# A fixed program order for four engines in the attention phase of an attention and two-MoE kernel

## The chip, the core and the metric

One core of one Trainium2 chip runs the whole kernel. It has a matrix engine (TensorE, "PE" in the rows, with its weight loads as "PEld"), a vector engine (VectorE, "DVE"), a scalar engine (ScalarE, "ACT"), GpSimd ("POOL") and SyncE ("SP", which here only issues DMAs). Each engine works through its own list of instructions in the order in which the built program has them, and waits at an instruction until its inputs and its output buffer are ready. The metric is the device time of one run in microseconds (us), lower is better.

## What is computed

Three blocks follow one another: top-32 attention over 4 batches, 8 heads and 576 positions (head size 64), a dense feed-forward block with a hard gate, and a sparse block of 8 experts with two experts per token. All is fp32.

```python
scores = scale * q @ k.T
kth = np.partition(scores, -32, axis=-1)[..., -32:-31]
attn = softmax(where(scores >= kth, scores, -1e9))
x = (attn @ v), laid out as 2304 tokens x 512
h = x @ w_in                       # 512 -> 2048
x = (h * clip(h + 3, 0, 6) / 6) @ w_out
logits = x @ w_gate + log1p(exp(x @ w_noise)) * noise
out = sum over the two best experts of weight * (relu(x @ w1[e]) @ w2[e])
```

## The kernel before, in words

`phase_a` does the attention and the dense block together, `phase_b` the experts. The 2304 query rows are 18 tiles of 128; a tile and a head make one "slot" of work, 144 in all, and the loop `for st in range(-6, end)` at the end of `phase_a` is a software pipeline over slots. In its step `st` it calls, each for another slot: the key and query transposes and their copies (`k_trans`, `kq_trans`, `k_evac`, `q_evac`) for slot st; the scores on PE and their copy to SBUF on ACT (`scores`, `s_evac`) and seven segment maxima on DVE (`seg`, L313) for slot st-1; the threshold search over the segment maxima (`chain`, L319 to L323), the bias for the exponential on POOL (`nbias`) and the mask (`zmask`, L340) for st-2; the product of mask and scores on POOL (`ysum`, L346) and the exponential on ACT for st-3; the exact 32nd value (`ymax` L352, `select` L356) and the masked sum (`pmask`, L365, `recip`) on DVE for st-4; the transposes of the result on PE (`ptrans`, with `ptevac` on ACT) for st-5; the product with the values (`av`, one call per two heads) for st-6; and the scaling and rounding of the result (`xscale`, `xsplit`) later.

The dense block runs in the same loop as "units": a chunk of 256 tokens and one of 16 blocks of 128 hidden columns. There are 144 units, one per step from step 25 on, so the last 25 run after the attention. A unit is `mm1` (12 matmuls into one PSUM bank, tile `h`), `hrelu` on ACT, `hgate` on DVE (L478), and in the next step `hround` on ACT, `hlow` on POOL (L491) and `mm2` (6 matmuls, tile `xa`). Bank `h` exists once: `mm1` of a unit waits for `hgate` of the unit before. Its weights arrive as 64-bit numbers. In the steps 4 to 19 one block of them per step is converted (`convert`, four DVE instructions, L117 and L118 twice, one on ACT, one on POOL) and split (`split`: PE and ACT); 11 of the 16 blocks are written back and streamed again for every chunk.

The keys of a batch and head are loaded, split and transposed once, shortly before the first slot that needs them (`ksched`): heads in 4 runs of 8 steps. As a batch has 4.5 tiles, 16 slots (tiles 4 and 13) hold rows of two batches and need twice the score matmuls.

When the last units of a chunk are done, the routing for the experts (`make_route`) comes as a list of small closures of which a few are called at the end of each step; `logits` are 4 transposes and `logits2` the small matmuls that follow, one of them per step, four steps a chunk.

What sets the order: the kernel is recorded in the order of the loop, but the tile framework's scheduler then builds each engine's list by its own model of time and by priorities. Two places guide it by hand: `av` raises the priority of its matmuls (`AVP_AHEAD`) and `after` chains a few instructions. Ring sizes are the constants at the top (`KTB` for transposed keys, `VB` for values, `VL` the step at which values are loaded); PSUM is full, each tag once.

Of the kernel before, what the change touches and what calls it, by code (L numbers as in the profile page):

```python
# [30 lines left out]
WD = 2  # L31
WP = 16
LAG = 10
AVP_AHEAD = 150
ZB = 2
OS, OA, OB, OC, OD, OE, OV, OX, OY = 1, 1, 2, 3, 4, 5, 6, 8, 10
VL = 4
SSB = 4

ONV = ''  # L40
# [2 lines left out]
BEGIN = 12  # L43
KRB = 2
LXB = 2
VB = 9
XMB = 2
QRB = 2
GB = 2
KTB = 10  # L50
PHB = 2
SEGB = 3
A8B = 4
# [87 lines left out]


def phase_a(tc, pools, ident, q, k, v, w_in, w_out, X, thrs, wscr, stream, begin, on_chunk=None, slots=NSLOT, pace=None):
    nc = tc.nc
    wp, ap, mp, ps, dr = pools
    TS, TT, STT = nc.vector.tensor_scalar, nc.vector.tensor_tensor, nc.vector.scalar_tensor_tensor

# [48 lines left out]
    KT, V = {}, {}  # L196

    KR, KS = {}, {}

    def k_load(i):  # L200
        dl, b, h = ksched[i]
        KR[i] = kr = ap.tile([128, 5, 64], F32, name=f"kr{i}", tag="kr", bufs=KRB)
        nc.sync.dma_start(kr[:, 0:4, :], k[b, h, 0:512, :].rearrange("(p j) d -> p j d", j=4))
        nc.sync.dma_start(kr[0:64, 4, :], k[b, h, 512:576, :])

    def k_split(i):

        kr = KR.pop(i)
        KS[i] = ks = ksb[i % KSB]
        for sl in ((slice(0, 128), slice(0, 4)), (slice(0, 64), slice(4, 5))):  # L210
            hi, lo = ks[sl[0], sl[1], 0, :], ks[sl[0], sl[1], 1, :]
            copy('k', hi, kr[sl])
            nc.gpsimd.tensor_tensor(lo, kr[sl], ks.bitcast(F32)[sl[0], sl[1], 0, :], op=ALU.subtract)

    def v_load(i):
        dl, b, h = ksched[i]
        vt = ap.tile([128, 5, 64], F32, name=f"v{i}", tag="v", bufs=VB)
        nc.sync.dma_start(vt[:, 0:4, :], v[b, h, 0:512, :].rearrange("(p j) d -> p j d", j=4))
        half = slice(64 * (h % 2), 64 * (h % 2) + 64)
        nc.sync.dma_start(vt[half, 4, :], v[b, h, 512:576, :])  # L220
        other = 64 - 64 * (h % 2)
        nc.gpsimd.memset(vt[other:other + 64, 4, :], 0.0)
        V[b, h] = vt

    KP, QP = {}, {}

    def k_trans(i):
        ks = KS[i].rearrange("p j a d -> p j (a d)")
        pm = ps.tile([128, 512], F32, name=f"kp{i}", tag="pa")
        for j in range(4):  # L230
            flip(nc, pm[:, j * 128:(j + 1) * 128], ks[:, j, :], identr)
        KP[i] = pm

    def kq_trans(i, t):
        pm = ps.tile([128, 512], F32, name=f"qp{i}_{t}", tag="misc")
        if t is not None:
            qs = QS[divmod(t // 4, 2)][:, t % 4].rearrange("p a d -> p (a d)")
            flip(nc, pm[:, 0:128], qs[:, 0:128], identr)
            flip(nc, pm[:, 128:256], qs[:, 128:256], identr)
            QP[t] = pm  # L240
        if i is not None:
            ks = KS.pop(i)[:, 4].rearrange("p a d -> p (a d)")
            flip(nc, pm[:, 256:384], ks, identr)
            KP[i] = (KP[i], pm)

    def k_evac(i):
        dl, b, h = ksched[i]
        KT[b, h] = kt = ap.tile([128, 576], F32R, name=f"kt{i}", tag="kt", bufs=KTB)
        p0, p1 = KP.pop(i)

        m, r = (0, 512) if h % 2 == 0 else (64, 0)
        copy('K', kt[:, m:m + 512], p0)
        copy('K', kt[:, r:r + 64], p1[:, 256:320])
# [138 lines left out]
    def ptevac(i):  # L392
        p = PP.pop(i)
        if i % 2:
            p, half = p
            PH[i // 2] = ap.tile([128, 128], F32, name=f"ph{i}", tag="pth", bufs=PHB)
            first = nc.scalar.copy(PH[i // 2], half)  # L397
        PT[i] = ap.tile([128, 4, 128], F32, name=f"pt{i}", tag="ptt", bufs=PTB)
        last = nc.scalar.copy(PT[i], p.rearrange("p (a n) -> p a n", a=4))
        if i % 2: after(tc, last, first)  # L400

    PH = {}
    AVP, RP, XS, XT = {}, {}, {}, {}
# [1 line left out]
    def av(p):  # L405

        t = p // 4
        AVP[p] = o = ps.tile([128, 512], F32, name=f"av{p}", tag="av")
        prev = None
        with tc.high_priority(AVP_AHEAD):  # L410
            for b, row, n, s0 in pieces(t):
                for j in range(5):
                    for hh in (1, 0):
                        half = slice(64 * hh, 64 * hh + 64)
                        vt, pt = V[b, (2 * p + hh) % 8][:, j, :], PT[2 * p + hh][:, j, :] if j < 4 else PH[p]
                        m = nc.tensor.matmul(o[half, row:row + n], vt, pt[:, row:row + n], start=(j == 0),  # L416
                                             stop=(j == 4), skip_group_check=True)
                        if prev: after(tc, m, prev)
                        prev = m
            m = nc.tensor.transpose(o[:, 128:256], RB.pop(p).rearrange("p a b -> p (a b)"), ident)  # L420
            after(tc, m, prev)
# [110 lines left out]
    wstep = {}  # L532
    for fb in range(NFB):
        wstep.setdefault(W0 + fb * WD // 2, []).append(fb)
    kdl = {dl: i for i, (dl, b, h) in enumerate(ksched)}
    for st in range(-6, end):
        if st == -6: q_load(0, 0)
        if st == BEGIN: begin()
        if st % 4 == 0 and 0 < st // 4 + 1 < slots // 4: q_load(*divmod(st // 4 + 1, 2))
        if st % 4 == 2 and 0 <= st // 4 + 1 < slots // 4: q_split(*divmod(st // 4 + 1, 2))  # L540
        for i, (dl, b, h) in enumerate(ksched):
            if max(dl - 3, min(i, 2) - 6) == st: k_load(i)
            if max(dl - 1, min(i, 2) - 5) == st: k_split(i)
            if dl + VL == st: v_load(i)
        for fb in wstep.get(st + 2, []): wk.load(fb)

        while fetched < len(units) and units[fetched][0] <= st + 3:
            w_fetch(units[fetched][1]); fetched += 1
        u, up = ustep.get(st), ustep.get(st - 1)
        s_, a, b, c, d, e, av_, x1, x2 = (st - x for x in (OS, OA, OB, OC, OD, OE, OV, OX, OY))  # L550
        if ok(x1) and x1 % 2 == 0: xscale(x1 // 2)
        if up:
            hround(up)
            hlow(up)
        if ok(c):
            ysum(c)
            expo(c)
        if u:
            mm1(u)
            hrelu(u)  # L560
        if ok(s_): scores(s_)
        if ok(e): ptrans(e)
        if ok(s_): s_evac(s_)
        if ok(e): ptevac(e)
        ki = kdl.get(st)
        if ki is not None: k_trans(ki)
        if ki is not None or ok(st):
            kq_trans(ki, st if ok(st) else None)
        if ki is not None: k_evac(ki)
        if ok(st): q_evac(st)  # L570

        ch = chain(b) if ok(b) else []
        segs = [(a, j) for j in range(NSEG)] if ok(a) else []
        if ok(d): ymax(d)
        if ch:
            ch.pop(0)()
            nbias(b)
        if ok(d): select(d)
        while ch:
# [681 lines left out]
```

## Time and profile before

| what | us |
|---|---|
| median of three runs (lowest 1414.99, highest 2076.86) | 1418.17 |
| the profiled execution, its own time | 1414.92 |
| its span in the profile | 1413.0 |
| PE busy in the span | 1301.9 |
| VectorE busy in the span | 1000.8 |
| GpSimd busy in the span | 828.6 |
| ScalarE busy in the span | 744.6 |

All times of the trace count from the start of the span; 1.9 us of the execution lie outside it. The attention's last mask ends just before 836 us, the experts follow from about 906 us. A busy share is an average over stages: PE's and VectorE's shares are close to full in the attention, and VectorE's falls behind it.

### The profile page before, as it was taken

The page shows a single profiled execution, that of the slowest core. Times are in us where ns is not written, and L with a number is a line of the kernel's source. Part 1 is how long each engine was busy: PE and PEld are TensorE (multiplying, and loading weights), DVE is VectorE, ACT ScalarE, POOL GpSimd, SP SyncE. Part 2 cuts the span into 40 slices and gives each one's busy share as a digit, 9 for nine tenths or more (in the row PEclk, how much of TensorE's full clock was granted, in tenths as well). Part 3 has the DMA queues.
Part 4 walks back from the last instruction along what each step waited for, and adds up shares of the span by engine and source line. Part 5 has one row for each costly group of instructions (what it writes and reads, how often), then busy time and mean ns, then how long its engine had stood idle before and what let it go on. Part 6 is the DMA issues. An engine that isn't in the chain of part 4 may idle for free.

```text
span 1413.0 us, 26990 instructions
## 1 busy us (share of the span) xinstructions
PE 1301.9 (92%) x9006; PEld 1129.0 (80%) x9006; DVE 1000.8 (71%) x3805; ACT 744.6 (53%) x1565; POOL 828.6 (59%) x1173
## 2 busy tenths in 40 slices
PE   5767899999999979999899999799999999999996
PEld 3545688988888868898688888677989888888985
DVE  7999997899998899986899973345453534444241
ACT  6767766677676756666676654244322322223220
POOL 7665666666666778665577864234414556465461
PEclk8789999999999989999999999999999999999999
DMA  8766645445345614445233547556546556474431
GB/s 244 257 237 226 239 171 193 146 152 172 130 178 191 223 14 156 164 168 200 70 128 137 149 148 256 174 173 224 168 137 195 169 172 192 140 222 163 145 121 38
DMA packets 138100, 239.56 MB, mean 170 GB/s; under 512 B 39779, under 2 KB 93155, under 8 KB 123872
## 3 DMA queue, kind: packets, MB, share of 16 engines
q1 hardware_dynamic: 127600, 210.57, 45.2%
q0 software_dynamic: 10352, 27.18, 5.8%
q8 instruction: 73, 1.20, 0.4%
q14 instruction: 75, 0.61, 0.1%
HBM read 209.08 MB, written 31.64 MB: 170 GB/s over the span
## 4 chain that ended last, share of the span: by engine, by line
PE 56%; DVE 26%; POOL 5%; ACT 4%; DMA 4%; issue 3%; SPq 1%; POOLq 0%; DVEq 0%; ACTq 0%
PE hb L876 15%; PE ac L896 15%; PE h L463 8%; PE xa L503 7%; DVE seg L313 5%; DVE e L365 5%; DVE a L352 4%; DVE z L340 3%; PE s L295 3%; PE av L416 3%; PE pa L384 2%; DVE a L356 2%; DMA kr<-in_k_dram 1%; POOL idw L756 1%; DVE r L478 1%
## 5 line engine op out<-in xcount | busy, mean ns | idle before, releaser
L896 PE MATMUL ac<-w,hh 128*128 128x512 f32 x960 | 247.5, 400 | 4.6 <-ACT hh L881 4.5
L876 PE MATMUL hb<-xe,w 128*128 128x320 f32 (+2 forms) x1536 | 239.4, 310 | 1.1 <-DVE xe L846 0.4
L876 PEld LDWEIGHTS hb<-xe,w 128*128 128x128 f32 x1536 | 231.7, 189 | 9.9 <-issue 3.0
L346 POOL TENSOR_TENSOR y<-z,ss 128x576 f32<-128x576 bf16 x144 | 192.4, 1337 | 57.6 <-DVE z L340 51.3
L896 PEld LDWEIGHTS ac<-w,hh 128*128 128x128 f32 x960 | 173.1, 188 | 43.8 <-ACT hh L881 8.4
L882 DVE SCALAR_TENSOR_TENSOR hh<-hb,hh 128x640 fp32r<-128x640 f32 (+2 forms) x72 | 53.9, 749 | 211.2 <-ACT hh L881 199.7
L881 ACT ACTIVATE hh<-hb 128x640 fp32r<-128x640 f32 (+2 forms) x72 | 46.6, 647 | 293.1 <-PE hb L876 270.2
L313 DVE MAX8 seg<-ss 128x8 f32<-128x82 f32 (+1 forms) x1008 | 166.8, 228 | 21.0 <-ACT ss L304 20.6
L463 PE MATMUL h<-xT,ws 128*128 128x256 f32 x1188 | 164.5, 287 | 7.6 <-DVE r L478 7.4
L503 PE MATMUL xa<-ws,g 128*128 128x512 f32 x594 | 165.8, 403 | 0.0
L463 PEld LDWEIGHTS h<-xT,ws 128*128 128x128 f32 x1188 | 149.6, 190 | 15.1 <-DVE r L478 12.6
L862 POOL TENSOR_TENSOR w<-r,w 128x1024 fp32r<-128x1024 f32 x40 | 98.2, 2462 | 85.1 <-ACT w L860 77.7
L365 DVE SCALAR_TENSOR_TENSOR e<-ss,thrs,e 128x576 f32<-128x576 f32 x144 | 141.7, 984 | 0.5
L335 ACT ACTIVATE e<-ss,a 128x576 f32<-128x576 f32 x144 | 114.0, 792 | 34.4 <-POOL a L328 33.3
L304 ACT COPY ss<-s 128x576 f32<-128x576 f32 x144 | 92.6, 643 | 66.1 <-PE s L389 47.1
L352 DVE MAX8 a<-y 128x8 f32<-128x576 f32 x144 | 108.0, 750 | 25.0 <-POOL y L346 24.8
L491 POOL TENSOR_TENSOR g<-r,g 128x256 fp32r<-128x256 f32 x124 | 96.5, 778 | 36.5 <-ACT g L187 23.2
L340 DVE TENSOR_SCALAR_CACHE_REDUCE z<-ss,a 128x576 bf16<-128x576 f32 x144 | 115.3, 801 | 1.0
L384 PE MATMUL pa<-ident,e 128*128 128x128 f32 x576 | 93.2, 286 | 24.7 <-DVE e L365 21.1
L503 PEld LDWEIGHTS xa<-ws,g 128*128 128x128 f32 x594 | 102.1, 188 | 14.7 <-POOL g L491 0.5
L295 PE MATMUL s<-kt,qt 128*128 128x288 f32 x512 | 102.3, 324 | 8.7 <-ACT ph L397 4.2
L913 POOL DMA_INDIRECT out_dram<-y,id x40 | 42.3, 1058 | 104.1 <-DVE y L912 82.5
(195 smaller groups left out, 2655.3 us busy)
## 6 DMA issues: line engine op xcount, KB each, us to landing
ws<-wscr SPq DMA_DIRECT2D x99, 1024.0 KB
r<-in_moe_w_dram SPq DMA_DIRECT2D x144, 256.0 KB
wscr<-wsp SPq DMA_DIRECT2D x11, 1024.0 KB
wraw<-in_moe_w_in_dram SPq DMA_DIRECT2D x16, 512.0 KB
wraw<-in_moe_w_out_dram SPq DMA_DIRECT2D x16, 512.0 KB
ck<-in_moe_w_in_dram SPq DMA_DIRECT2D x32, 256.0 KB
ck<-in_moe_w_out_dram SPq DMA_DIRECT2D x32, 256.0 KB
out_dram<-zero SPq DMA_DIRECT2D x18, 256.0 KB
```

The costliest lines, as they stand in the source:

```text
L295: nc.tensor.matmul(p[:, half, 0:288], qt[:, j, :], KT[b, h][:, half * 288:(half + 1) * 288], start=(m == 0), stop=(m == n - 1))
L313: nc.vector.max(ST[i][:, j, :], SS[i][:, edge[j]:edge[j + 1]])
L335: nc.scalar.activation(e, SS[i], AF.Exp, bias=A8[i][:, 24:25], scale=0.125)
L340: TS(z, SS[i], A8[i][:, 7:8], None, op0=ALU.is_lt, op1=ALU.add, accum_out=A8[i][:, 26:27])
L346: nc.gpsimd.tensor_tensor(y, Z.pop(i), SS[i], op=ALU.mult)
L352: nc.vector.max(A8[i][:, 8:16], Y.pop(i))
L365: STT(E[i], SS.pop(i), thrs[:, i:i + 1], E[i], op0=ALU.is_ge, op1=ALU.mult, accum_out=SUM[i // 2][:, i % 2:i % 2 + 1])
L384: nc.tensor.transpose(p[:, j * 128:(j + 1) * 128], e[:, j * 128:(j + 1) * 128], ident)
L463: nc.tensor.matmul(p[:, 0:n], w[:, a, d, :], xt[b][:, d, 0:n], start=(m == 0), stop=(m == 11))
L503: nc.tensor.matmul(ACC[t], g[:, a, j * 128:(j + 1) * 128], w[:, b, :], start=(fb == 0 and m == 0), stop=(fb == NFB - 1 and m == 2))
L876: nc.tensor.matmul(p[:, half, 0:hn], w[:, a, d, :], XE[job][:, b, d, half * hn:(half + 1) * hn], start=(m == 0), stop=(m == 11))
L896: o = nc.tensor.matmul(ACC[job, j], h[:, a, j * 128:(j + 1) * 128], w[:, b, :], start=(f == 0 and m == 0), stop=(f == NF2 - 1 and m == 2))
```

## The change

`phase_a` gets its engines from a wrapper, `Lanes`. Each of PE, DVE, ACT and POOL is a `Lane` that adds an ordering edge from every instruction to the one recorded before it on the same engine, so that in `phase_a` (and in the weight conversion that it calls) the scheduler can no longer reorder them. Only SP's DMAs and the closures of `make_route` stay free and are placed between them. The calls in a step are laid out anew: scores first, then the first matmuls of a unit; keys are split two steps ahead, transposed one step ahead (`kdl` has `dl - 1`, `k_trans` after `mm2`) and loaded four ahead; values are loaded one step later; `hgate` comes before the mask. The rings of keys and values get one more buffer each, the priority for `av` goes. As `ptrans` now comes after `s_evac`, the fifth transpose of an odd head gets a PSUM tile of its own turn (`s{i}x`) instead of a corner of the current scores.

```diff
-AVP_AHEAD = 150
-VL = 4
+VL = 5
-VB = 9
+VB = 10
-KTB = 10
+KTB = 11
+class Lane:
+    def __getattr__(self, name):
+        f = getattr(self.engine, name)
+        def call(*args, **kw):
+            o = f(*args, **kw)
+            if self.last is not None:
+                after(self.tc, o, self.last)
+            self.last = o
+            return o
+        return call
 def phase_a(...):
-    nc = tc.nc
+    nc = Lanes(tc)
 ...
-    kdl = {dl: i for i, (dl, b, h) in enumerate(ksched)}
+    kdl = {dl - 1: i for i, (dl, b, h) in enumerate(ksched)}
     for st in range(-6, end):
-        if st % 4 == 2 and 0 <= st // 4 + 1 < slots // 4: q_split(*divmod(st // 4 + 1, 2))
-            if max(dl - 3, min(i, 2) - 6) == st: k_load(i)
-            if max(dl - 1, min(i, 2) - 5) == st: k_split(i)
-            if dl + VL == st: v_load(i)
+            if max(dl - 4, min(i, 2) - 6) == st: k_load(i)
...
-        if ok(x1) and x1 % 2 == 0: xscale(x1 // 2)
+        ki = kdl.get(st)
         if up:
             hround(up)
             hlow(up)
+        if ok(s_):
+            scores(s_)
+            s_evac(s_)
         if ok(c):
             ysum(c)
             expo(c)
         if u:
             mm1(u)
             hrelu(u)
-        if ok(s_): scores(s_)
-        if ok(e): ptrans(e)
-        if ok(s_): s_evac(s_)
-        if ok(e): ptevac(e)
-        ki = kdl.get(st)
-        if ki is not None: k_trans(ki)
+        if ok(e):
+            ptrans(e)
+            ptevac(e)
         if ki is not None or ok(st):
             kq_trans(ki, st if ok(st) else None)
-        if ki is not None: k_evac(ki)
         if ok(st): q_evac(st)
+        if ok(x1) and x1 % 2 == 0: xscale(x1 // 2)
...
         if segs: seg(*segs.pop(0))
+        if u: hgate(u)
         if ok(b): zmask(b)
         if ok(d):
             pmask(d)
-        if u: hgate(u)
+        while segs: seg(*segs.pop(0))
         if ok(d) and d % 2 == 1: recip(d // 2)
-        while segs: seg(*segs.pop(0))
         if up:
             mm2(up)
+        if ki is not None:
+            k_trans(ki)
+            k_evac(ki)
         if ok(av_) and av_ % 2: av(av_ // 2)
+            if dl + VL == st: v_load(i)
         if ok(x2) and x2 % 2 == 0: xsplit(x2 // 2)
+        if st % 4 == 2 and 0 <= st // 4 + 1 < slots // 4: q_split(*divmod(st // 4 + 1, 2))
+            if max(dl - 2, min(i, 2) - 5) == st: k_split(i)
         for fb in wstep.get(st, []): w_split(fb)
         for fb in wstep.get(st + 1, []): wk.convert(fb)
```

In the rows of the changed kernel all wrapped instructions carry line 85, the wrapper's call.

How the instructions move shows at three places. On DVE at the program's start (wt and wraw belong to the conversion of weights, seg, a8 and z to the attention, the number is that of the block or head), before:

```order
L117 TENSOR_SCALAR wt0_0_345<-wraw0_239 128x512
L118 SCALAR_TENSOR_TENSOR wraw0_239<-wraw0_239,wt0_0_345 128x512
L117 TENSOR_SCALAR wt0_1_348<-wraw0_239 128x512
L118 SCALAR_TENSOR_TENSOR wraw0_239<-wraw0_239,wt0_1_348 128x512
L313 MAX seg0_163<-ss0_161 128x8 x7
L319 MAX a80_216<-seg0_163 128x8
L320 MATCH_REPLACE seg0_163<-a80_216,seg0_163 128x56
L321 MAX a80_216<-seg0_163 128x8
L117 TENSOR_SCALAR wt1_0_430<-wraw1_297 128x512
```

and in the changed kernel the first conversion stands behind the third mask:

```order
L85 MAX seg3_313<-ss3_311 128x8
L85 TENSOR_SCALAR z2_337,a82_323<-ss2_260,a82_323 128x576
L85 SCALAR_TENSOR_TENSOR e0_265,sum0_339<-ss0_174,thrs_71,e0_265 128x576
L85 MAX seg3_313<-ss3_311 128x8 x2
L85 TENSOR_SCALAR wt0_0_355<-wraw0_252 128x512
L85 SCALAR_TENSOR_TENSOR wraw0_252<-wraw0_252,wt0_0_355 128x512
L85 TENSOR_SCALAR wt0_1_358<-wraw0_252 128x512
```

The conversions have moved from ahead of the first head to behind the fourth step of the attention; five blocks stood ahead of the third mask before, none does now.

On DVE in the middle of the attention, around head 90 (a8, z, e and y of a head as in the words above, r4 the dense block's chunk 4), before:

```order
L356 SCALAR_TENSOR_TENSOR a888_7868,thrs_71<-rank_85,a888_7868 128x9
L478 SCALAR_TENSOR_TENSOR r4_5_8184<-r4_5_8184,h4_5_8171 128x256
L340 TENSOR_SCALAR z89_7960,a889_7946<-ss89_7856,a889_7946 128x576
L323 MAX a890_8039<-seg90_7938 128x8
L365 SCALAR_TENSOR_TENSOR e88_7909,sum88_8055<-ss88_7757,thrs_71,e88_7909 128x576
L340 TENSOR_SCALAR z90_8053,a890_8039<-ss90_7936,a890_8039 128x576
L313 MAX seg91_8029<-ss91_8027 128x8 x7
L371 RECIPROCAL sum86_7884<-sum86_7884 128x2
L478 SCALAR_TENSOR_TENSOR r4_6_8260<-r4_6_8260,h4_6_8247 128x256
```

and one whole step of the changed kernel, which repeats for every slot:

```order
L85 MAX a888_7910<-y88_7959 128x8
L85 MAX a890_8084<-seg90_7958 128x8
L85 SCALAR_TENSOR_TENSOR a888_7910,thrs_71<-rank_85,a888_7910 128x9
L85 MAX seg91_8046<-ss91_8044 128x8
...
L85 MAX a890_8084<-seg90_7958 128x8
L85 MAX seg91_8046<-ss91_8044 128x8
L85 SCALAR_TENSOR_TENSOR r4_3_8063<-r4_3_8063,h4_3_8050 128x256
L85 TENSOR_SCALAR z90_8099,a890_8084<-ss90_7956,a890_8084 128x576
L85 SCALAR_TENSOR_TENSOR e88_7961,sum88_8101<-ss88_7776,thrs_71,e88_7961 128x576
L85 MAX seg91_8046<-ss91_8044 128x8 x2
```

Two masks and two gates stand within nine rows before; now there is one of each per step, and the gate of unit 3 of the chunk stands where unit 5 and 6 stood.

On POOL at the same heads (g is `hlow`, y is `ysum`, idw a routing scatter), before:

```order
L491 TENSOR_TENSOR g4_4_8165<-r4_4_8092,g4_4_8165 128x256
L756 DMA idw_76<-pl0_6276,ix0_6277 18432x2 x2
L370 TENSOR_SCALAR sum86_7884<-sum86_7884 128x2
L328 TENSOR_SCALAR a890_8039<-a890_8039 128x1
L268 TENSOR_TENSOR qsb1_102<-qr12_1_8331,qsb1_102 128x4x64
L346 TENSOR_TENSOR y89_7998<-z89_7960,ss89_7856 128x576
```

and now:

```order
L85 TENSOR_SCALAR sum86_7927<-sum86_7927 128x2
L85 TENSOR_SCALAR rb43_8012<-sum86_7927 128x128
L85 TENSOR_TENSOR g4_2_8036<-r4_2_7976,g4_2_8036 128x256
L85 TENSOR_TENSOR y89_8047<-z89_8005,ss89_7870 128x576
L783 DMA idw_76<-pl0_6315,ix0_6316 18432x2 x2
L85 TENSOR_TENSOR xs42_8081<-xs42_8081 128x128
```

In the changed kernel g and y of a step stand back to back at the step's start, with the scatters behind or between them.

## Rows read from the trace of the kernel before

**Rows 1.** Windows: stretch and length, busy us (instructions) by engine, PEclk, DMA share, GB/s.

```profile
0.00:35.00 35.00, 19.63 (x67) 12.06 (x67) 26.51 (x70) 24.35 (x49) 25.53 (x56) 0.89 0.82 243
212.00:836.00 624.00, 592.24 (x4882) 525.28 (x4881) 560.46 (x2573) 420.83 (x1002) 427.38 (x723) 0.98 0.46 151
495.00:530.00 35.00, 25.94 (x204) 21.83 (x203) 33.99 (x156) 19.86 (x46) 25.47 (x39) 0.85 0.12 13
600.00:672.00 72.00, 71.50 (x574) 65.02 (x573) 52.18 (x214) 45.82 (x123) 41.86 (x71) 1.00 0.55 186
706.00:777.00 71.00, 67.82 (x562) 60.25 (x562) 70.51 (x339) 50.81 (x115) 53.41 (x97) 1.00 0.38 131
```

**Rows 2.** Groups of instructions, 212 to 836 us: count, busy us, mean ns, idle before.

```profile
L340 DVE TENSOR_SCALAR_CACHE_REDUCE z<-ss,a 128x576 bf16<-128x576 f32 x112 | 89.8, 802 | 1.0
L472 ACT ACTIVATE r<-h,three 128x256 f32<-128x256 f32 x111 | 53.2, 479 | 27.1 <-PE h L463 25.3 <-POOL rt L702 0.6 <-POOL a L328 0.4
```

**Rows 3.** The same view, 706 to 777 us, the masks.

```profile
L340 DVE TENSOR_SCALAR_CACHE_REDUCE z<-ss,a 128x576 bf16<-128x576 f32 x15 | 12.0, 799 | 0.0
```

**Rows 4.** Chain that ended last, around 302 us: start, us, what.

```profile
302.52 1.48 PE h L463 x12
...
306.89 0.53 PE s L295 x4
...
312.04 0.19 PE h L463
```

**Rows 5.** The same chain, 640 to 672 us.

```profile
639.91 0.56 PE lg L672 x5
...
653.12 0.29 PE kp L73 x4
...
656.28 0.79 PE s L295 x6
...
660.70 0.26 PE s L295 x2
```

**Rows 6.** The same chain, 831 to 862 us.

```profile
831.55 1.79 DVE e L365 x2
...
834.96 0.72 DVE z L340 x2
...
861.17 0.44 PE lt L661 x4
```

**Rows 7.** Who waited for whom, 212 to 848 us: total us, times, longest.

```profile
ACT ss L304 <- PE s L389: 29.5, 30, 3.7
...
DVE a L352 <- POOL y L346: 24.8, 23, 3.4
```

**Rows 8.** Instructions by line, whole span: ns shortest/median/longest.

```profile
L356 DVE SCALAR_TENSOR_TENSOR a<-rank,a x144: 201/229/2641, 24.0 to 838.6; 128x9 f32<-128x9 f32 x144
```

**Rows 9.** The same for the masked sum.

```profile
L365 DVE SCALAR_TENSOR_TENSOR e<-ss,thrs,e x144: 790/816/2753, 24.6 to 838.9; 128x576 f32<-128x576 f32 x144
```

**Rows 10.** Groups of VectorE, 212 to 848 us.

```profile
L365 DVE SCALAR_TENSOR_TENSOR e<-ss,thrs,e 128x576 f32<-128x576 f32 x114 | 107.2, 940 | 0.5
...
L356 DVE SCALAR_TENSOR_TENSOR a<-rank,a 128x9 f32<-128x9 f32 x114 | 42.0, 368 | 1.0 <-ACT e L335 0.7
```

**Rows 11.** Timeline around 574 us: start, us, engine, instruction.

```profile
574.06 1.29 POOL L346 TENSOR_TENSOR y<-z,ss 128x576 f32<-128x576 bf16 x1 [0.52 <-DVE z L340]
...
574.74 0.64 DVE L356 SCALAR_TENSOR_TENSOR a<-rank,a 128x9 f32<-128x9 f32 x1
```

**Rows 12.** Timeline of VectorE from the start.

```profile
8.13 0.64 DVE L117 TENSOR_SCALAR wt<-wraw 128x512 int32<-128x512 int32 x1 [5.02 <-DMA wraw<-in_moe_w_in_dram]
...
11.69 1.12 DVE L313 MAX8 seg<-ss 128x8 f32<-128x82 f32 x7 [0.60 <-ACT ss L304]
```

**Rows 13.** Groups of instructions, 0 to 212 us: the conversion on VectorE.

```profile
L118 DVE SCALAR_TENSOR_TENSOR wraw<-wraw,wt 128x512 int32<-128x512 int32 x32 | 24.9, 780 | 0.1
L117 DVE TENSOR_SCALAR wt<-wraw 128x512 int32<-128x512 int32 x32 | 23.7, 740 | 9.1 <-DMA wraw<-in_moe_w_in_dram 8.7 <-DMA wraw<-in_moe_w_out_dram 0.4
```

More of the change, by code (lines that the diff above doesn't have):

```diff
@@ L73, in flip, with __init__, __getattr__ @@
     nc.tensor.transpose(out.bitcast(F32R), in_, identr)
+class Lane:
+    def __init__(self, tc, engine):
+        self.tc, self.engine, self.last = tc, engine, None
+    def __getattr__(self, name):
[7 more added lines that the diff above has]
+        return call
+class Lanes:
+    def __init__(self, tc):
+        self.nc = tc.nc
+        self.tensor, self.vector, self.scalar, self.gpsimd = (
+            Lane(tc, e) for e in (tc.nc.tensor, tc.nc.vector, tc.nc.scalar, tc.nc.gpsimd))
+    def __getattr__(self, name):
+        return getattr(self.nc, name)
 class Weights:
@@ L223, in v_load @@
         V[b, h] = vt
-    KP, QP = {}, {}
+    KP, KH, QP = {}, {}, {}
     def k_trans(i):
-        ks = KS[i].rearrange("p j a d -> p j (a d)")
+        ks = KS.pop(i).rearrange("p j a d -> p j (a d)")
         pm = ps.tile([128, 512], F32, name=f"kp{i}", tag="pa")
@@ L241, in kq_trans @@
         if i is not None:
-            ks = KS.pop(i)[:, 4].rearrange("p a d -> p (a d)")
+            ks = KS[i][:, 4].rearrange("p a d -> p (a d)")
             flip(nc, pm[:, 256:384], ks, identr)
-            KP[i] = (KP[i], pm)
+            KH[i] = pm
     def k_evac(i):
@@ L248, in k_evac @@
         KT[b, h] = kt = ap.tile([128, 576], F32R, name=f"kt{i}", tag="kt", bufs=KTB)
-        p0, p1 = KP.pop(i)
+        p0, p1 = KP.pop(i), KH.pop(i)
         m, r = (0, 512) if h % 2 == 0 else (64, 0)
@@ L396, in ptevac @@
             PH[i // 2] = ap.tile([128, 128], F32, name=f"ph{i}", tag="pth", bufs=PHB)
-            first = nc.scalar.copy(PH[i // 2], half)
+            nc.scalar.copy(PH[i // 2], half)
         PT[i] = ap.tile([128, 4, 128], F32, name=f"pt{i}", tag="ptt", bufs=PTB)
-        last = nc.scalar.copy(PT[i], p.rearrange("p (a n) -> p a n", a=4))
-        if i % 2: after(tc, last, first)
+        nc.scalar.copy(PT[i], p.rearrange("p (a n) -> p a n", a=4))
     PH = {}
@@ L408, in av @@
         AVP[p] = o = ps.tile([128, 512], F32, name=f"av{p}", tag="av")
[L409 to L421, printed above, removed]
+        for b, row, n, s0 in pieces(t):
+            for j in range(5):
+                for hh in (1, 0):
+                    half = slice(64 * hh, 64 * hh + 64)
+                    vt, pt = V[b, (2 * p + hh) % 8][:, j, :], PT[2 * p + hh][:, j, :] if j < 4 else PH[p]
+                    nc.tensor.matmul(o[half, row:row + n], vt, pt[:, row:row + n], start=(j == 0),
+                                     stop=(j == 4), skip_group_check=True)
+        nc.tensor.transpose(o[:, 128:256], RB.pop(p).rearrange("p a b -> p (a b)"), ident)
     def xscale(p):
@@ L592, in phase_a @@
             if up[1] == NFB - 1: xout(up[0])
+        if ki is not None:
+            k_trans(ki)
+            k_evac(ki)
         if ok(av_) and av_ % 2: av(av_ // 2)
+        for i, (dl, b, h) in enumerate(ksched):
+            if dl + VL == st: v_load(i)
         if ok(x2) and x2 % 2 == 0: xsplit(x2 // 2)
+        if st % 4 == 2 and 0 <= st // 4 + 1 < slots // 4: q_split(*divmod(st // 4 + 1, 2))
+        for i, (dl, b, h) in enumerate(ksched):
+            if max(dl - 2, min(i, 2) - 5) == st: k_split(i)
         for fb in wstep.get(st, []): w_split(fb)
```

## The prediction

> **What bounds the kernel now.** I read the windows first, to find the stage that the change can reach, then the counts of work in it, then the chain of waits, and last the durations of the instructions that move. The change touches `phase_a` alone, so the stretch that counts runs to the last mask, at 834.96 + 0.72 = 835.7 us, say 836 [rows 6]. From 212 to 836 us the reader should look at two columns: PE is busy 592.24 of 624 us and VectorE 560.46 [rows 1]. Both are near full and neither is full. In these 624 us 112 heads are masked and 111 units of the dense block pass [rows 2], so a slot, one head with one unit, takes 624 / 112 = 5.57 us.
>
> What a slot needs at least can be read where one engine was never late. On PE the chain runs for whole slots through PE alone: unit to unit, two slots, from 302.52 to 312.04 us [rows 4], 4.76 us a slot. On VectorE the stretch from 706 to 777 us is busy 70.51 of 71 us [rows 1] with 15 masks [rows 3]; some of its first and last head lies outside, so 14 to 15 heads, 4.70 to 5.04 us a slot. I take the middle, 4.86 us.
>
> So 5.57 us are paid where the larger engine needs about 4.9. The loss shows as an alternation. From 495 to 530 us VectorE is busy 33.99 of 35 us while PE has 25.94 and its granted clock falls to 0.85, between the two levels of 1.2 and 2.4 GHz, after PE had gone idle; from 600 to 672 us PE is busy 71.50 of 72 us and VectorE only 52.18 [rows 1]. The scheduler's order lets the dense units run ahead of the attention and then fall behind it, and each engine waits while the other has its turn. A fixed order, one unit and one head per step, removes that drift.
>
> **Part by part.** *The order in the middle.* The change removes no arithmetic. I sort the 112 heads of 212 to 836 us into four kinds of step and give each the larger of its two engines.
>
> Plain steps, 60: VectorE is the larger, 4.86 us. In that number some waiting on POOL is already in. A two-input instruction of VectorE stretches when a POOL instruction is running: the product y starts at 574.06 and lasts 1.29, to 575.35; the small selection starts at 574.74 and lasts 0.64, to 575.38, instead of its median of 0.229 [rows 8, 11]. Over the stage the selection averages 0.368 and the masked sum 0.940 against medians of 0.229 and 0.816 [rows 8 to 10], together 0.26 us a slot. In the new order g and y stand back to back at the step's start on POOL, and the selection is the third instruction of VectorE's step, so it meets them often. Bounds: 0.26 less if it never does, up to a whole y, 1.3, more if it always does; I take 0.2 more, nearer to the average of today: 5.05 us.
>
> The Trainium skill, "SBUF — State Buffer", section "Who interferes with whom", states that VectorE's second SBUF input uses a port shared with GpSimd, held for a whole instruction, the other engine blocked. The trace agrees (0.64 for 0.229 in the row just named). By that rule alone every meeting costs the rest of the POOL instruction; that outcome is the second rival below, priced from rows.
>
> Steps in which a routing closure uses PE, 28 (7 chunks, 4 steps): two sets of 4 transposes at 0.44 [rows 6] and two of 8 small matmuls at 0.56 / 5 = 0.11 each [rows 5] are 2.7 us a chunk, 0.67 a step. PE needs 4.76 + 0.67 = 5.43; I take 5.45.
>
> Steps with rows of two batches, 16: the scores are 8 matmuls, 0.79 + 0.26 against 0.53 us [rows 4, 5]; the keys' transposes, 0.29 [rows 5], fall into nearly the same steps; with an allowance of 0.15 for the extra flip and the pieces of `av`, PE needs 4.76 + 0.52 + 0.29 + 0.15 = 5.7. The copies of new keys stand at the end of ACT's step, so some of it couples: 5.9. Steps with new keys alone, 8: 4.76 + 0.35 = 5.1; I take 5.3.
>
> The sum is 60 x 5.05 + 28 x 5.45 + 16 x 5.9 + 8 x 5.3 = 303 + 153 + 94 + 42 = 592 us against 624: 32 us gained. The lower bound is PE without a gap: 112 x 4.76 + 28 x 0.67 + 16 x 0.96 + 8 x 0.35 = 571 us. The upper is the second rival.
>
> By the column of busy time PE would have only 32 us to give (624 - 592). The Trainium skill, "Perfetto Trace Analysis", "Identifying the Most-Contended Engine", says that matmul busy time is no measure of what is left, because matmuls are pipelined. The chain bears that out here: 571, not 592, is PE's need.
>
> *The own PSUM tile of the fifth transpose.* Before, the copy of the scores waited for that transpose, 29.5 us in all [rows 7], and the segment maxima behind it. That goes. Late next is y, for which VectorE waits 24.8 us now [rows 7]; in the new order y is made a step before its reader. So this part is what allows 5.05 and gets no term of its own; at worst it is worth nothing, as ACT is not full (420.83 of 624 us [rows 1]).
>
> *The waits that the order adds.* Behind a waiting instruction the whole lane queues. `hgate` waits for `hrelu` of the same step; behind it stand the mask and the masked sum. The chain there is scores 0.53, `mm1` 1.48 [rows 4] and `hrelu` 0.48 [rows 2], about 2.7 us with handovers; VectorE reaches `hgate` about half way through its step of 5.05, with 12 of some 18 instructions ahead of it. So it costs nothing once PE's step starts a little ahead of VectorE's, which bank `h` allows: it is free again when the gate of the step before is done, and PE asks for it only after the scores. `k_split` at the end of ACT's and POOL's step waits for the keys' DMA; `hround` and `hlow` of the next step stand behind it. Its load is now issued two steps, some 10 us, ahead, as before, so I cost it at nothing; without that cover each late load would stop both lanes. On SP, whose order stays free, key loads go one step earlier and value loads one later past the weight stream; no term.
>
> *The start.* The conversions of weights wait behind the third mask now. Before, VectorE did the first at 8.13 us, ahead of the first segment maxima at 11.69 [rows 12]; of the first 35 us it was busy 26.51 [rows 1]. A block costs 2 x 0.740 + 2 x 0.780 = 3.04 us [rows 13], and five stood ahead of the third mask, 15 us. That work moves later, onto an engine that is full then. If the first heads come no sooner for it, 15 us are lost; if VectorE's idle time is filled with heads instead, nothing is, and the conversion no longer waits for its DMA (9.1 us [rows 13]), a gain of at most that. I take 7 us lost, about half of the larger end.
>
> *After 836 us* nothing moves: the last chunk's units, the routing and the experts keep their order; 1414.9 - 836 = 579 us.
>
> Sum: 212 + 7 + 592 + 579 = **1390 us**, 25 below the profiled execution's 1414.92, or 1.8%. That execution is 3.3 us below the median of the runs, 1418.17, so against the median the same change would read about 1393. About 2% is what a measurement of this kernel can tell from no change.
>
> **The rivals.** *A: the order is better than that, PE runs without gaps.* For it: the rings are sized for it and each input is made a step ahead. Against it: VectorE's 4.86 is itself above PE's 4.76. With 576 us in the middle and nothing lost at the start: 212 + 576 + 579 = 1367.
>
> *B: POOL and VectorE block each other in every step.* The place is the selection and the masked sum beside y and g. The uncontended slot is 4.86 - 0.26 = 4.60; one whole y a slot, 1.29, gives 5.9, and 112 x 5.9 = 661 us: 212 + 7 + 661 + 579 = 1459. It loses from the point at which the stretch passes 5.57 - 4.60 = about 1 us a slot, four times today's. For it: g and y stand back to back, at the same point of each step. Against it: today's instructions meet as well and pay 0.26.
>
> *C: the lanes wait for one another and the slot stays at 5.57.* One late input (a key's DMA, a PSUM bank used by routing and by the query transposes) stops everything behind it, where the scheduler would have had something else in front. 212 + 7 + 624 + 579 = 1422. For it: VectorE has 10% and PE 5% of idle time today [rows 1], so little is needed to keep all of it; against it: the largest wait of VectorE today is 24.8 us in all [rows 7], and that one goes.
>
> That the order isn't fixed at all can be left out: the changed rows on VectorE repeat step by step.
>
> **How the numbers follow.** The forecast, with its own range of 1375 to 1408, gets 0.48, of which 0.18 lies below the line of 2% (1386.6) and 0.30 above. A gets 0.24, faster; C 0.14, the same; B 0.14, slower. So faster 0.18 + 0.24 = 0.42, same 0.30 + 0.14 = 0.44, slower 0.14. For 8 in 10 the range runs from 1360, 7 us under A for a start that gains, to 1432, 10 us over C; B's and a little of A's and C's chance stay out.
>
> **What would show it.** Right: masks and gates one for one at every point of the stage; 112 masks in about 592 us; the window shares of VectorE and PE both above 93% with no stretch as that from 600 to 672 us; no clock below 1.0 there; the score copy no longer waiting for the fifth transpose. The start right: the 32nd mask some 7 us later. Wrong: a mean of the selection above 0.8 us (B), idle time of VectorE before the segment maxima or the gate of more than 0.4 us a slot (C), or a time after the last mask that isn't 579 us.

## The result: slower by 1.3%

The changed kernel takes 1437.39 us (median; 1429.88 to 1440.31) against 1419.37 us of the kernel before beside it, a ratio of 1.0128 with a 95% interval of 1.0110 to 1.0146. The profiled execution's span is 1435.7 us. The prediction was 1390 us, in a range of 1360 to 1432.

All runs are cut at the same two marks, the ends of the 32nd and the 144th mask z. Of the 22.7 us that the span grew, the start lost 29.1, the middle gained 22.7 and the part behind the last mask lost 16.3:

| span in us, cut at the marks | start, to 32nd mask | middle, 112 masks | behind the last mask | span |
|---|---|---|---|---|
| before | 211.2 | 624.5 | 577.3 | 1413.0 |
| predicted | 219 | 592 | 579 with what lies outside the span | |
| changed | 240.3 | 601.8 | 593.6 | 1435.7 |

Windows of the changed kernel, columns as in [rows 1]; the first, fourth, fifth and sixth line answer to rows there, and the others are its three stages:

```profile
0.00:35.00 35.00, 15.43 (x71) 12.66 (x71) 17.19 (x71) 19.39 (x47) 17.87 (x48) 1.00 0.71 207
0.00:240.00 240.00, 166.89 (x910) 118.64 (x911) 188.48 (x753) 149.43 (x301) 131.14 (x207) 0.85 0.59 195
240.00:842.00 602.00, 583.65 (x4874) 518.54 (x4872) 546.78 (x2565) 419.22 (x1003) 418.86 (x724) 0.99 0.47 157
495.00:530.00 35.00, 33.09 (x266) 27.75 (x265) 34.99 (x170) 22.45 (x53) 24.40 (x48) 1.00 0.43 152
600.00:672.00 72.00, 70.78 (x603) 64.64 (x602) 60.27 (x285) 53.44 (x145) 47.50 (x84) 1.00 0.48 162
706.00:777.00 71.00, 68.85 (x559) 60.83 (x558) 66.78 (x320) 51.44 (x116) 50.25 (x94) 1.00 0.46 159
842.00:1435.70 593.70, 559.65 (x3224) 494.95 (x3223) 241.34 (x489) 175.81 (x262) 260.98 (x243) 0.98 0.51 165
```

In the middle PE is busy 97% (583.65 of 602). The stretch 495 to 530 us has lost its starved PE (25.94 before, 33.09 now). In the first 35 us VectorE is busy 17.19 us, where it was 26.51: the first conversions are gone from there, and no heads have come in their place. VectorE waits.

For whom, the waits of the changed kernel from 0 to 212 us show (all wrapped instructions carry L85):

```profile
DVE seg L85 <- ACT ss L85: 45.4, 12, 11.2
POOL wraw L85 <- ACT wraw L85: 44.3, 9, 12.1
PEld wp L85 <- ACT wsp L85: 35.2, 11, 10.9
ACT wsp L85 <- DMA wscr<-wsp: 24.2, 4, 11.1
```

Three engines wait for ScalarE, and ScalarE for a DMA: `wsp` is a split weight block, `wscr` the copy of it in DRAM. The chain that ended last, at the second such block, and ScalarE's timeline there:

```profile
48.91 7.55 DMA wscr<-wsp
...
56.54 1.12 ACT wsp L85
...
61.74 0.53 ACT ss L85
```

```profile
51.43 0.41 ACT L85 CAST qt<-qpNone 128x256 fp32r<-128x256 f32 x1
56.54 1.11 ACT L85 CAST wsp<-wraw 128x1024 fp32r<-128x1024 f32 x1 [4.70 <-DMA wscr<-wsp]
...
61.65 0.62 ACT L85 COPY ss<-s 128x576 f32<-128x576 f32 x1
```

Weight blocks come into, are split in and are streamed through one ring of four buffers (`NSTR`). A split needs a buffer of the ring, and ScalarE's copy into it is released only when the write-back of the block before, 7.55 us, has ended. ScalarE stands from 51.8 to 56.5 us, the next score copy is queued behind that, and with it VectorE's segment maxima and every other lane.

### The profile page after: what moved, and what is told of

It is laid out like the page before. It is cut to its first block, busy times and chain, and to the rows that moved or that the text cites. A ratio compares the mean times of both kernels' runs of the same rounds, so it can differ in the third digit from the quotient of the medians.

```text
span 1435.7 us, 27207 instructions
## 1 busy us (share of the span) xinstructions
PE 1310.2 (91%) x9006; PEld 1132.1 (79%) x9006; DVE 976.6 (68%) x3805; ACT 744.5 (52%) x1565; POOL 811.0 (56%) x1173
## 4 chain that ended last, share of the span: by engine, by line
PE 66%; DVE 11%; DMA 7%; POOL 6%; ACT 5%; issue 3%; SPq 2%; POOLq 0%; ACTq 0%; DVEq 0%
PE ac L923 15%; PE hb L903 15%; PE xa L85 10%; PE h L85 9%; PE av L85 5%; PE s L85 4%; DVE seg L85 3%; DVE a L85 3%; PE wp L85 2%; PE pa L85 2%; DMA wscr<-wsp 2%; POOL idw L783 2%; DVE e L85 1%; DVE z L85 1%; PE et L869 1%
## 5 line engine op out<-in xcount | busy, mean ns | idle before, releaser
L85 DVE MAX8 seg<-ss 128x8 f32<-128x82 f32 (+1 forms) x1008 | 221.6, 232 | 83.6 <-ACT ss L85 82.8
L903 PE MATMUL hb<-xe,w 128*128 128x320 f32 (+2 forms) x1536 | 239.4, 311 | 3.0 <-ACT xe L872 1.2
L85 POOL TENSOR_TENSOR y<-z,ss 128x576 f32<-128x576 bf16 x144 | 188.3, 1308 | 0.3 <-DVE z L85 0.3
L85 PE MATMUL xa<-ws,g 128*128 128x512 f32 x594 | 164.5, 408 | 8.1 <-POOL g L85 7.8
L85 PE MATMUL h<-xT,ws 128*128 128x256 f32 x1188 | 160.0, 284 | 1.3 <-DVE r L85 1.3
L85 ACT COPY ss<-s 128x576 f32<-128x576 f32 x144 | 92.3, 641 | 122.6 <-PE s L85 73.4
L85 PEld LDWEIGHTS h<-xT,ws 128*128 128x128 f32 x1188 | 150.8, 191 | 4.3 <-DVE r L85 3.0
L85 PEld LDWEIGHTS xa<-ws,g 128*128 128x128 f32 x594 | 102.0, 188 | 31.4 <-POOL g L85 15.9
L85 DVE SCALAR_TENSOR_TENSOR e<-ss,thrs,e 128x576 f32<-128x576 f32 x144 | 123.0, 854 | 0.0
L85 ACT ACTIVATE e<-ss,a 128x576 f32<-128x576 f32 x144 | 112.7, 783 | 8.1 <-POOL a L85 8.1
L85 DVE TENSOR_SCALAR_CACHE_REDUCE z<-ss,a 128x576 bf16<-128x576 f32 x144 | 115.4, 801 | 0.0
L85 DVE MAX8 a<-y 128x8 f32<-128x576 f32 x144 | 106.9, 742 | 0.0
L85 PE MATMUL s<-kt,qt 128*128 128x288 f32 x512 | 103.4, 327 | 3.2 <-ACT qt L85 3.0
L85 PEld LDWEIGHTS s<-kt,qt 128*128 128x128 f32 x512 | 86.5, 213 | 16.3 <-issue 6.5
L85 POOL TENSOR_TENSOR xs<-xs 128x128 f32<-128x128 f32 x72 | 50.7, 705 | 85.4 <-ACT xs L85 85.2
```

The source lines that it names most:

```text
L85: o = f(*args, **kw)
L903: nc.tensor.matmul(p[:, half, 0:hn], w[:, a, d, :], XE[job][:, b, d, half * hn:(half + 1) * hn], start=(m == 0), stop=(m == 11))
```

## The experiments

First the stages of all runs. Start, middle and behind are those of one profiled execution, median and ratio (to the kernel before, measured beside each) are over several; three of the profiled executions lie off their median by more than 4 us: e3 (1387.70), e5 (1404.55) and b1 (1412.29).

| run | start | middle | behind | median us | ratio, 95% interval |
|---|---|---|---|---|---|
| e1 order from step 26 | 206.0 | 599.7 | 590.4 | 1398.40 | 0.9885, 0.9867 to 0.9903 |
| e2 order to step 25 | 239.4 | 613.3 | 578.8 | 1431.33 | 1.0102, 1.0085 to 1.0119 |
| e3 layout, no order | 206.7 | 599.8 | 579.3 | 1393.99 | 0.9852, 0.9833 to 0.9871 |
| e4 weights free | 215.1 | 600.1 | 590.1 | 1406.81 | 0.9933, 0.9916 to 0.9950 |
| w2 split free | 216.8 | 599.1 | 589.5 | 1408.13 | 0.9956, 0.9935 to 0.9977 |
| w3 conversion free | 237.8 | 599.0 | 589.0 | 1429.55 | 1.0125, 1.0092 to 1.0157 |
| w5 order, five buffers | 217.2 | 599.0 | 592.0 | 1410.90 | 0.9953, 0.9925 to 0.9981 |
| b2 before, five buffers | 208.1 | 624.5 | 583.0 | 1416.23 | 1.0000, 0.9985 to 1.0015 |
| k1 keys in own step | 203.4 | 617.1 | 578.8 | 1399.41 | 0.9898, 0.9873 to 0.9924 |
| p1 shared tile | 204.5 | 605.6 | 582.2 | 1393.23 | 0.9853, 0.9828 to 0.9879 |
| a1 priority back | 208.1 | 606.5 | 581.2 | 1400.60 | 0.9866, 0.9819 to 0.9912 |
| b1 before, no priority | 207.3 | 614.1 | 589.1 | 1404.87 | 0.9883, 0.9834 to 0.9932 |
| e5 order in 26 to 149 | 205.4 | 599.6 | 597.8 | 1399.94 | 0.9849, 0.9801 to 0.9896 |
| c1 layout, five buffers | 212.2 | 594.7 | 588.0 | 1396.24 | 0.9855, 0.9833 to 0.9878 |
| e3 again | 208.7 | 601.3 | 577.6 | 1390.51 | 0.9811, 0.9790 to 0.9831 |

**Where in the program: e1 to e4.** Edits of the changed kernel: a switch in `Lane.call`, set per step (e1 and e2), no wrapper (e3), the plain engines for the weights (e4).

```diff
-            self.last = o
+            if Lane.on: self.last = o
+        Lane.on = st >= 26      # e1;  st < 26 in e2
-    nc = Lanes(tc)
+    nc = tc.nc                  # e3
-    wk = Weights(nc, ...)
+    wk = Weights(tc.nc, ...)    # e4
```

e1: 

> The new layout of calls, with the fixed order only from step 26 on; steps -6 to 25 (attention's first 24 heads and all weight blocks) are left to the scheduler. Stages by the 32nd and the 144th mask: before 211, 836, 1413; changed kernel 240, 842, 1436. Theory 1 (the fixed order costs its time at the start, where each weight block waits in line on ScalarE and GpSimd, and gains in the middle): 32nd mask at 205 to 215, 600 us from there to the last mask, in all 1395 to 1410. Rival 2 (the new layout of calls costs the start, not the order): 32nd mask at 235 or later, in all 1430 or more. Rival 3 (a head start is given back, since something after the start sets the end): 32nd mask near 211, but the middle 620 or more, in all 1425 or more.

e2: 

> The fixed order in steps -6 to 25 only; behind it, on each engine, the scheduler is free, on the new layout of calls. Theory 1: start lost (32nd mask near 240), middle as before (about 624), in all 1435 to 1455. Rival 2 (the layout, not the order, makes both the loss and the gain): middle near 602, in all about 1430 to 1436. Rival 3: 1415 to 1425, since the middle takes the loss back.

e3: 

> The new layout of calls, rings and distances, without any fixed order. Theory 1: start and middle near those of before (211, 624), in all 1405 to 1425. Rival 2: 32nd mask at 235 or later and a middle near 602, in all 1425 to 1436.

e4: 

> The changed kernel, but the conversion and the split of the weight blocks (their instructions on VectorE, ScalarE, GpSimd and TensorE) are not part of the fixed order; everything else is, in all steps. Theory 1: most of the 29 us at the start come back, 32nd mask at 211 to 222, middle near 602, in all 1400 to 1418. If the start is lost by the order of the attention's own instructions: 32nd mask stays at 235 to 240, in all 1430 to 1436.

The start depends on the order alone: 206 and 207 us without, 239 with. With only the weights free it is 215. So theory 1 holds there. In the middle it falls: e3 has no order and the same 600 us as e1, and its time lies below what either theory expected of it. What removed the alternation is the new layout of calls; the order itself gains nothing (0.9885 with it from step 26, 0.9852 without). The middle of e2, 613 us, fits neither theory, since it has more work in it. Its ordered start leaves it behind with the dense units, and it makes that up: 1377 matmuls of `mm1` pass in its middle, 1335 in that of e3, 3.5 units. By the busy times of `mm1` in e3 (191.95 us) and of `mm2` in the changed kernel (187.57 us for 672) a unit takes PE 3.4 us, so these are some 12 of the 13.5 us, as an estimate. The window of e2's middle, and those of e3's middle, two of the stretches above and its end:

```profile
239.40:852.70 613.30, 606.19 (x4941) 528.08 (x4939) 570.14 (x2574) 425.75 (x1005) 434.66 (x721) 1.00 0.48 157
```

```profile
207.00:806.00 599.00, 590.34 (x4866) 517.06 (x4865) 563.45 (x2556) 418.98 (x995) 426.60 (x715) 1.00 0.48 156
600.00:672.00 72.00, 72.00 (x667) 64.77 (x666) 65.13 (x276) 50.54 (x125) 47.15 (x78) 1.00 0.45 149
706.00:777.00 71.00, 66.95 (x530) 57.83 (x529) 68.03 (x322) 48.71 (x109) 55.82 (x95) 0.98 0.41 139
807.00:1385.80 578.80, 552.17 (x3171) 489.30 (x3169) 242.95 (x483) 174.00 (x256) 258.73 (x239) 0.98 0.52 168
```

e3's PE is busy 590.34 of 599 us with the clock at 1.00, and VectorE has 65.13 in the stretch where [rows 1] has 52.18 and the changed kernel 60.27.

**Which half of the weight work: w2, w3.** Here `split`, or `convert`, alone takes its instructions from the plain engines.

```diff
     def split(self, fb, w, on_pe):
-        nc = self.nc
+        nc = self.nc.nc         # w2; the same line of convert in w3
```

w2: 

> The changed kernel, with only the split of the weight blocks (ScalarE, TensorE, two copies out of PSUM) taken out of the fixed order; the conversion stays in it, behind the third mask. With both out, the 32nd mask came at 215 and the time was 1407; with both in, 240 and 1437. Theory 1a (the split is what holds the start up: its first copy waits on ScalarE for the write-back of the block before, 24 us in four waits, and score copies stand behind it): 32nd mask at 212 to 224, in all 1403 to 1416. Theory 1b (the conversion's late place holds it up): 32nd mask at 232 or later, in all 1426 or more.

w3: 

> The other half: the conversion is out of the fixed order, the split stays in it. Theory 1a: 32nd mask at 230 or later, in all 1425 to 1437. Theory 1b: 32nd mask at 212 to 222, in all 1403 to 1415. If each half costs its own share, both this and the run with the split free lie near 225 and 1420.

The split costs the start 240.3 - 216.8 = 23.5 us, the conversion's late place 240.3 - 237.8 = 2.5. Theory 1a.

**The wait itself: w5 and its control b2.** All order kept; five buffers in the ring, paid for with one resident block less.

```diff
-NRES = 5
-NSTR = 4
+NRES = 4
+NSTR = 5
```

w5: 

> The changed kernel with five buffers instead of four in the ring that raw weights, split blocks and streamed weights share, and with four resident blocks instead of five (so 12 blocks are written back and streamed). Theory 1c (the split waits for the write-back of the block before because the ring is full): that wait goes, 32nd mask at 215 to 225, in all 1405 to 1422. Rival (the split stalls the start by its chain from engine to engine, whatever the buffers): 32nd mask at 233 or later, in all 1428 or more.

b2 (the same two lines in the kernel before): 

> Control for the run with five ring buffers and four resident blocks (1411 against 1437 of the changed kernel): the same two sizes in the kernel before, whose scheduler puts other work ahead of a split that would wait (it waits 1.4 us for write-backs). Theory 1c (the ring helps only where a fixed order queues behind the wait): 1410 to 1424, ratio to before 0.995 to 1.005. Rival (five buffers help any order, since streamed weights come earlier): 1390 to 1402, as much as the 26 us they gave the changed kernel.

ScalarE's timeline of w5 at the place shown above:

```profile
51.56 0.40 ACT L85 CAST qt<-qpNone 128x256 fp32r<-128x256 f32 x1
52.02 1.13 ACT L85 CAST wsp<-wraw 128x1024 fp32r<-128x1024 f32 x1
...
56.42 0.62 ACT L85 COPY ss<-s 128x576 f32<-128x576 f32 x1
```

The split no longer waits, and the score copy comes 5.2 us sooner. Over 0 to 240 us, ScalarE's idle time before these copies, in the changed kernel and in w5:

```profile
L85 ACT CAST wsp<-wraw 128x1024 fp32r<-128x1024 f32 x11 | 12.4, 1128 | 24.4 <-DMA wscr<-wsp 24.2
```

```profile
L85 ACT CAST wsp<-wraw 128x1024 fp32r<-128x1024 f32 x12 | 13.7, 1138 | 0.9 <-POOL wraw L85 0.6
```

23.5 us of waiting went (24.4 - 0.9) and 23.1 us of the start (240.3 - 217.2). In the kernel before these copies hardly waited, from 0 to 212 us:

```profile
L130 ACT CAST wsp<-wraw 128x1024 fp32r<-128x1024 f32 x11 | 12.9, 1169 | 1.4 <-DMA wscr<-wsp 1.4
```

There the same two sizes change nothing in all (ratio 1.0000; its start is 208.1 where it was 211.2). So the buffer's wait is the cause of these 23 us, and it costs them only where a fixed order queues behind it.

**What the layout gains by: k1, p1, a1, b1.** Each undoes one part of e3: keys as before (k1); `ptrans` ahead of `s_evac` (p1); the priority of `av` back, with the edges that chained its matmuls (a1). b1 is the kernel before without that priority and those edges.

```diff
-kdl = {dl - 1: i ...}; k_load at dl - 4, k_split at dl - 2, k_trans behind mm2
+kdl = {dl: i ...}; k_load at dl - 3, k_split at dl - 1, k_trans behind kq_trans   # k1
-scores(s_); s_evac(s_); ...; ptrans(e); ptevac(e)
+scores(s_); ptrans(e); s_evac(s_); ...; ptevac(e)                                 # p1
-        with tc.high_priority(AVP_AHEAD):                                         # b1, put back in a1
```

k1: 

> The new layout without a fixed order (1394 in the run before, ratio 0.985), but with the keys as before: loaded three steps, split one step ahead, transposed and copied in the step of their first slot ahead of the queries' copy. Theory L1 (keys ahead of time are what the layout gains): 1408 to 1417, with the 600 us between the 32nd and the 144th mask back at 615 to 625. Theory L2 (the gain is the place of the scores and of the fifth transpose): 1391 to 1398.

p1: 

> The new layout without a fixed order, but the transposes of the result stand between the scores and their copy again, so that the fifth transpose of an odd head goes into the current score tile and the copy waits for it. Theory L2: 1408 to 1417, and the score copy waits some 30 us for the fifth transpose again. Theory L1: 1391 to 1398.

a1: 

> The new layout without a fixed order (1394, ratio 0.985), with the raised priority of the value matmuls and the edges among them put back as before. Theory L3 (that priority is what made the dense units and the heads alternate): 1405 to 1417, with stretches again in which VectorE is busy 75% and TensorE full. Otherwise 1390 to 1398.

b1: 

> The kernel before with nothing changed but the value matmuls' raised priority and the edges among them taken away. Theory L3: it gets most of the layout's 22 us: 1393 to 1404. Otherwise 1412 to 1422.

The fifth transpose's own tile is worth nothing (0.9853 without it, 0.9852 with it). The keys are worth part: 0.9898 lies between what the two theories expected, and the middle takes 617 us again. Taking the priority away gives the kernel before most of the gain, 0.9883 (interval to 0.9932) and just over the 1393 to 1404 of theory L3, yet putting it back costs the new layout nothing that the intervals show (1400.60 lies between its two expectations). Nor is it what makes units and heads alternate, as L3 has it: without it VectorE is busy 54.23 of the 72 us from 600 on in b1, and with it 65.56 in a1. Of the three parts undone in the new layout only the keys cost anything clear. Which of its other moves gains the rest (the place of the scores and of `hgate`, the later values, the longer rings) was not tried one by one and stays open.

**Behind the last mask: e5.** The order ends at step 149.

```diff
-            self.last = o
+            self.last = o if Lane.on else None
+        Lane.on = 26 <= st < 150
```

> The new layout with the fixed order in steps 26 to 149 only; the start and the last steps (the dense units after the last heads, with the routing between them) are free. Stage times so far, with the order from step 26 to the end: 206, 600, 590; with no order at all: 207, 600, 579. Theory T (the fixed order costs some 11 us in the last steps, where routing and the experts' first transposes have to be fitted between ordered units): 1384 to 1392, with 576 to 583 us after the last mask. Rival (the 11 us are the state in which the ordered middle leaves the units at the last mask, one unit fewer started): 1394 to 1401, 586 to 592 us after the last mask.

Theory T falls: 597.8 us (the rival's 586 to 592 is missed as well, in an execution 4.6 us above its median). The order of the last steps isn't what costs the time. Part of the loss is there at the last mask already. PE's groups of the changed kernel from 842 to 1022 us, and of the kernel before from 836 to 1000:

```profile
L85 PE MATMUL h<-xT,ws 128*128 128x256 f32 x192 | 27.0, 292 | 1.3 <-DVE r L85 1.3
...
L85 PE MATMUL h<-xT,w 128*128 128x256 f32 x84 | 11.2, 282 | 0.0
L869 PE MATMUL et<-ident,xg 128*128 128x128 f32 x51 | 9.2, 309 | 13.4 <-DMA xg<-X,id 13.4
```

```profile
L463 PE MATMUL h<-xT,ws 128*128 128x256 f32 x181 | 25.4, 290 | 2.1 <-DVE r L478 2.1
...
L463 PE MATMUL h<-xT,w 128*128 128x256 f32 x72 | 9.5, 281 | 0.0
L842 PE MATMUL et<-ident,xg 128*128 128x128 f32 x48 | 8.2, 299 | 8.9 <-DMA xg<-X,id 8.9
```

At 12 matmuls a unit, 276 / 12 = 23 units are left against 253 / 12 = 21. With the other groups (`xa` 145 against 138, `lg` 40 against 32, `av` 48 against 32) that is 7.5 us of PE work more than the kernel before has at that mark. The middle did not put it off; it stood there at the first mark. The matmuls of `mm1` (tile `h`, busy us of PE) up to the first mark and from there to the second, in the changed kernel and in the kernel before:

```profile
0.00:240.30 240.30, 14.38 (x108) 0.85 0.59 194
240.30:842.10 601.80, 179.85 (x1344) 0.99 0.47 157
```

```profile
0.00:211.20 211.20, 20.70 (x132) 0.87 0.67 228
211.20:835.70 624.50, 190.42 (x1343) 0.98 0.46 151
```

108 matmuls are 9 units, 132 are 11. The order ties the ninth unit to the step of the 32nd mask (the first stands in step 25, that mask in step 33), and the scheduler had let the units run two ahead. e1, whose start is free up to step 25, has 9 there too. 4.5 us more (13.4 - 8.9) are waits for the experts' gathered rows. The other 4 of 16.3 us are not accounted for, and part of the stage moves without any order: b1 and c1 take 589.1 and 588.0 us behind the mark with 21 units left, as in the kernel before.

**The best version.** e3 again: 

> The new layout without a fixed order once more, beside the other two on one chip: ratio 0.982 to 0.988 by the run before.

 and with the five buffers (c1): 

> The best version so far (new layout, no fixed order, ratio 0.985) with the five ring buffers. Theory 1c: no difference, ratio 0.980 to 0.990. Rival: 0.972 or less.

 The layout without any fixed order beats both kernels, at 0.9811 (just below what was expected of it) to 0.9852. The buffers add nothing: with them it is 0.9855, a little slower than the 0.9811 beside it.

## Why the prediction was wrong, point by point

- **"The waits that the order adds"** is the step that failed. It went through `hgate` and `k_split` and left out the split of the weights, which stands in the same lanes and needs a buffer of the ring. It was worth 23.5 us (w2) and was counted as none. In the trace before it hardly shows, since there the scheduler hides it (1.4 us). The row to ask for was the write-back's time against the time between two splits.
- **"The start", +7 us,** counted VectorE's conversions alone; their place costs 2.5 us (w3), inside the bounds given. The rest of the order costs some 6 to 8 (215.1 in e4 against 206.7 and 208.7 in the two runs of e3), which also was not in the sum; which of its edges does it stays open. With the split the start is 240.3, not 219.
- **The middle, 592 us,** came out as 601.8: right in sign, 10 short. VectorE's 4.86 us a slot is 546.78 / 112 = 4.88. Units and heads do run one for one (units begun at the 64th, 96th and 128th mask: 41, 73, 105). What was mis-sized are the kinds of step. Two stretches of the changed kernel, nine masks without routing or new keys, and the eight masks beside the transposes of eight new keys:

```profile
391.34:434.35 43.01, 42.45 (x342) 37.77 (x341) 43.00 (x203) 30.97 (x73) 29.94 (x50) 1.00 0.48 159
434.35:482.61 48.26, 45.29 (x377) 40.46 (x376) 38.64 (x184) 39.77 (x101) 35.54 (x68) 1.00 0.60 195
```

  The first is 4.78 us a slot, where the sum had 5.05, with VectorE never idle. The second is 6.03, where it had 5.3: two rounds of the routing's transposes and small matmuls fall into it, and the sum had kept these kinds apart. Between the ends of the masks 48 of the 112 slots take less than 4.95 us, 4.78 on average, and the other 64 take 5.82; the sum had 60 at 5.05 and 52 at 5.56.
- **The floor of 571** (its terms add up to 570), and with it rival A: none of these runs came near it (lowest middle 594.7). PE is busy 583.65 us here and 578.97 in e1's middle, for the same work within two instructions, so the busy time isn't the floor either. Plain steps do come down to 4.78 us, beside the chain's 4.76; how far the steps with routing and keys could come down is not shown.
- **The reason for it, "a fixed order removes that drift",** was wrong as a cause. The layout alone gives the 600 us (e3). And the sign given for it, both shares above 93% and no stretch as that from 600 to 672 us, came only in part: VectorE has 546.78 of 602 us, 91%, and 60.27 of 72 there. That the calls' new places, not the edges, would steer the scheduler out of the alternation was a rival that the prediction lacked.
- **The fifth transpose** "is what allows 5.05": p1 shows it worth nothing without the order. The wait was only replaced:

```profile
ACT ss L85 <- PE s L85: 72.2, 48, 3.8
...
DVE seg L85 <- ACT ss L85: 36.2, 35, 2.7
...
DVE sum L85 <- POOL sum L85: 13.4, 7, 4.0
```

  From 240 to 842 us the score copy now waits 72.2 us for the scores themselves, against 29.5 for the fifth transpose [rows 7], and the wait for y is gone. VectorE's idle time before the maxima and the gate (36.2 and 2.4 us) is 0.34 us a slot, under the 0.4 set for rival C. The last line is a wait that the sum lacks: VectorE's reciprocal waits for GpSimd's sums, 13.4 us (3.1 before).
- **Rival B** is out. Groups of VectorE, 240 to 842 us, answering to [rows 10]:

```profile
L85 DVE SCALAR_TENSOR_TENSOR e<-ss,thrs,e 128x576 f32<-128x576 f32 x112 | 93.4, 834 | 0.0
...
L85 DVE SCALAR_TENSOR_TENSOR a<-rank,a 128x9 f32<-128x9 f32 x112 | 59.4, 530 | 0.0
```

  The selection rose from 368 to 530 ns, the masked sum fell from 940 to 834: 0.056 us a slot more, where 0.2 was allowed and B asked for about 1.
- **"After 836 us nothing moves"** failed by 16.3 us: the last mask is a mark on VectorE, and PE's backlog at it is not the same in two orders. 7.5 us of it are the two units by which the order holds PE back from the first mark on, and other work left with them.

Together: 21 us at the start, 10 in the middle and 16 behind it turn 1390 into 1437.

## What to carry to other kernels

Before every engine is put into a fixed order, go through each instruction in it that takes a buffer from a ring and ask who gives it back; where that is a DMA, the whole lane waits with it, and a scheduler that was hiding the wait hides it no longer. One more buffer in the ring can be worth more than the order. Where a change both moves calls and fixes their order, measure the move without the order first, and compare stages at a mark on the engine that sets the end.

## What the runs showed of the hardware that was not expected

The release of a buffer by a 1 MB write-back took 7.55 to 7.80 us in the chain of the changed kernel, longer than a whole step of its middle, 5.4 us; ScalarE's longest single wait for one was 11.1 us.

And the conflict of VectorE and GpSimd moved rather than grew: the selection's median went from 229 [rows 8] to 492 ns, while the masked sum got shorter. The prediction expected the selection to meet y; it mostly meets the end of g (or of a key's or query's subtraction in that place), as here:

```profile
328.19 0.74 POOL L85 TENSOR_TENSOR g<-r,g 128x256 fp32r<-128x256 f32 x1
...
328.47 0.49 DVE L85 SCALAR_TENSOR_TENSOR a<-rank,a 128x9 f32<-128x9 f32 x1
...
328.89 1.30 POOL L85 TENSOR_TENSOR y<-z,ss 128x576 f32<-128x576 bf16 x1
```

The selection, about 230 ns long where GpSimd is idle, takes 0.49 us here and ends at 328.96, just after g (328.93); y begins in its last 0.07 us. The Trainium skill, "SBUF — State Buffer", section "Who interferes with whom", has one of the two engines blocked by the other's whole instruction. The trace agrees: the selection is done when g is. What it costs depends on which instruction meets which, and the sum over a slot here is 0.056 us.
